# W_down's gradient in parts, the last V turned into other tiles, and the first dO pass inside W_up's gradient

## The chip, the cores and the metric

The kernel runs on one core of a Trainium2 chip. A core has TensorE (PE, matrix products and transposes), VectorE (DVE), ScalarE (ACT), GpSimd (POOL) and SyncE (SP), each with its own instruction queue, and 16 DMA engines that move data between the device's memory and the on-chip memory SBUF. SyncE only issues DMAs; ScalarE and GpSimd issue some too, between their other work. Products land in PSUM, eight banks of which a product of 512 float32 columns fills one. The metric is the device time of one execution in microseconds (us); the median over runs counts.

## The reference

The kernel computes the forward result and eleven gradients of one transformer block (2048 rows of width 512, bfloat16). Cut to what matters:

```
h = layernorm(x) * (1 + ca) + sa             # sa, ca, ga, sb, cb, gb = silu(c) @ w_mod
x = x + ga * A(h)                            # A: 64 segments of 32 rows, 8 memory rows carried on
                                             #    from one segment to the next, 32 heads of 128
h = layernorm(x) * (1 + cb) + sb
x = x + gb * B(h)
B(h) = (sigmoid(h @ w_gate) * (h @ w_up)) @ w_down      # the GLU, inner width 1792
out, vjp = jax.vjp(f, x, mem0, Wq, Wk, Wv, Wo, w_gate, w_up, w_down, c, w_mod)
return out, vjp(grad_out)
```

## The kernel before, in words

The program is one stretch of straight code in stages that follow each other:

- **phase2**: the forward pass over the 64 segments (s = 0 to 63), in order, since each segment's first 8 output rows are the next one's memory. Q, K, V, the turned V, the probabilities and the attention output are stored to DRAM (QST, KST, VT, PS, OT, OSR), for the backward pass. V is turned by a DMA transpose into the one tile `VTr` (L951), except in the last segment, where TensorE turns it in three parts (`turn_v`, L866), VectorE copies the parts to `VTr`, and SP stores it (L990). `RAs` are two pairs of tiles (k and q) that take the projected rows of even and odd segments. At its end, the first rows of the GLU are loaded (`glu_load`).
- **phase3**, first half, the GLU: 16 tiles of 128 rows pass seven stages, s0 to s6, `run_pipeline` with the deepest stage first; so iteration `it` handles stage k of tile it - k, and `after(it)` follows. s0: residual, layernorm, `h2` and `db`. s1: both turned (`hdT`, a DMA transpose from tile 2 on). s2: gate (`sg`) and up (`u`) products, `hh = sg * u`. s3: `du`, `dg`; `hhT` by a DMA transpose. s4: the product with w_down; `duT`, `dgT` by DMA transposes. s5: the gradient of h2, then `da`, `dx1`. s6: sums of gradients, and the turned `da` (`daT`), stored to DAOT. Rows for the weight gradients go to DRAM (HHROWS, DGROWS, DUROWS, DBROWS, H2ROWS). w_down is turned in eight pieces of seven transposes in iteration 2 (`wdT_pieces`).
- W_down's gradient: 14 products `fc` of 128 rows of W_down, each 16 matmuls over the tiles (`wd_chunk`), from `hrs` (columns of HHROWS, three `fc` at a time) and `dbr` (DBROWS). Products 0 to 2 are made in iterations 19 to 21 of the GLU; the rest after it.
- **phase3**, second half: products 3 to 13 of W_down's gradient, then W_gate's and W_up's gradients (32 groups of 16 matmuls). Between them the four weights of the attention are turned, in 32 pieces of 16 transposes (`p4_weights_setup_pieces`, spread by `emit_setup`): a piece is loaded by SP to a staging slot, turned by TensorE into PSUM (`wtp`), and copied by VectorE or ScalarE.
- **phase4**: the backward pass over the segments, from 63 down to 0. Every segment projects dy with WoT (`col_pass`), and turns dO (`dOT`; `dOst` holds its rows). The 8 tail rows of four segments are projected together (`proj_b`, into `RBds`, then turned into `btd`), one group of four ahead; `dO_tails` moves them to rows 96 to 119 of `dOst` by three DMAs on GpSimd's queue.
- **phase5**: the gradients of the attention weights from the stored rows, and the last layernorm backward.

What sets the order. The compiler's planner orders the instructions of each engine and each DMA queue by their place in the program, by its own estimate of when their inputs are there, and it inserts the waits. `self.pin(i0, engines)` fixes the program's order for the instructions recorded since i0 on these engines; `pin_behind` puts them behind an earlier stage. phase2 and the loop of phase4 are fixed on all engines; in the GLU, VectorE is fixed throughout, TensorE and ScalarE up to iteration 2, SP not at all. Tiles are carved out of the same SBUF by pools, stage after stage: a tile of a new stage lies over tiles of earlier ones, and its first write waits until all of these are read for the last time, stores to DRAM included.

Two large tiles, `Wk` and `Wv`, are cut into parts that are used anew after phase2 (`flat`): in `Wk` lie w_gate and w_up, then `dbr` and `hr_0`, then `h2r`; in `Wv` lie w_down and the rings of the GLU's inputs (`ring_a`, `ring_dout`), then the two halves of `ring` with the rows for the weight gradients. WoT, WqT, WkT and WvT, `daq` and `dyT` are allocated from the other end of SBUF.

The loads of the backward loop's first segment, in program order: K and Q rows, the cleared tiles, OT, PS, VT; and then the first dO pass (two halves), `dO_tails`, its turns and the heads' tail columns.

Of the kernel before, what the change touches and what calls it, by code (L numbers as in the profile page):

```python
# [40 lines left out]
class K:  # L41
# [395 lines left out]
    def phase2(self):  # L437
# [15 lines left out]
        with ExitStack() as ctx:  # L453
# [349 lines left out]
            for s in range(NS):  # L803
# [184 lines left out]
                if s == NS - 1:  # L988
                    nc.gpsimd.dma_start(self.w_down, io["B_w_down"].rearrange("(fc p) d -> p fc d", p=128))
                    nc.sync.dma_start(self.VT[s], VTr[:])  # L990
# [86 lines left out]
    def phase3(self):  # L1077
# [9 lines left out]
        with ExitStack() as ctx:  # L1087
# [110 lines left out]
            late = []  # L1198

# [4 lines left out]
            def s2(j, st):  # L1204
                r0, r1 = j * 128, (j + 1) * 128
                hdT = st["hdT"]
                sg = sbp.tile([128, F], BF16, name="sg", bufs=2)
                u = sbp.tile([128, F], BF16, name="u", bufs=1)
# [20 lines left out]
                if j == NT - 1:  # L1229
                    last_hh.append(hh)  # L1230
# [96 lines left out]
            def s6(j, st):  # L1327
# [9 lines left out]
                nc.sync.dma_start(self.DAOT[j * nseg:(j + 1) * nseg].rearrange("s p c t -> p s (c t)"),  # L1337
# [13 lines left out]
            def load_hr(g):  # L1351
                w, n = min(384, F - 384 * g), NT if g else NT - 1
# [3 lines left out]
            last_hh = []  # L1356

            def wd_chunk(fc, ps, ot):
                for j in range(NT):
                    rows = last_hh[0][:, 0:384] if fc < 3 and j == NT - 1 else hrs[fc // 3][:, j, :]  # L1360
                    nc.tensor.matmul(ps[:], lhsT=rows[:, (fc % 3) * 128:(fc % 3) * 128 + 128], rhs=dbr[:, j, :],
                                     start=(j == 0), stop=(j == NT - 1))
# [29 lines left out]
            self.run_pipeline(NT, [first, second, s2, s3, s4, s5, s6], deepest_first=True, after=after)  # L1392
            self.pin(i0, [ET.DVE])
# [9 lines left out]
        with ExitStack() as ctx:  # L1403
# [3 lines left out]
            units = 3 * (FC - 3) + 8 * 2 * NCH * DC  # L1407
            n_setup, done = len(setup_pieces), [0]

            def emit_setup(n):  # L1410
                done[0] += n
                while setup_pieces and (n_setup - len(setup_pieces)) * units < done[0] * n_setup:
                    setup_pieces.pop(0)()
            h2r = self.flat(self.Wk, NT * D, NT * D).rearrange("p (j d) -> p j d", j=NT)
# [23 lines left out]
            for (rows, outw) in ((self.DGROWS, io["out_7"]), (self.DUROWS, io["out_8"])):  # L1438
                for ch in range(NCH):
# [13 lines left out]
                    if outw is io["out_7"] and ch == 0:  # L1453
                        self.get_db(cfg.NS // 4 - 1)
            while setup_pieces:
                setup_pieces.pop(0)()
        self.wvk_ctx.close()

    def p4_weights_setup_begin(self):
# [14 lines left out]
        self.das, self.dbs = {}, {}  # L1474

# [12 lines left out]
    def p4_weights_setup_pieces(self, ctx):  # L1488
# [3 lines left out]
        stg = ctx.enter_context(tc.tile_pool(name="p4stage", bufs=1, reuse_waits="tile"))  # L1492
# [3 lines left out]
        slots = [stg.tile([128, DC * HB * E], BF16, name=f"stage{i}") for i in range(2)]  # L1496
        slots = [t[:, :] for t in slots] + [self.flat(self.Wv, 2 * cfg.NT * 448, DC * HB * E)]
        np_ = [0]

        def slot(pat, **kw):  # L1500
            np_[0] += 1
            return slots[np_[0] % 3].rearrange(pat, **kw)
# [29 lines left out]
        for h0 in range(0, H, HB):  # L1532
            pieces.append(wo_piece(h0))
# [817 lines left out]
```

## Time and profile before

Three runs took 3033.78, 3037.5 and 3036.22 us, a median of 3036.22. The profiled execution took 3034.87 us, of which 3033.1 are the span from the first to the last instruction. Its stages (us from the span's start, borders at TensorE's first instruction of the stage):

| stretch | what | length | TensorE busy | clock |
|---|---|---|---|---|
| 0 to 29.35 | setup | 29.35 | 12.77 | 0.94 |
| 29.35 to 976.16 | phase2, 64 segments | 946.81 | 926.65 | 0.99 |
| 976.16 to 1314.75 | GLU, products 0 to 2 of W_down's gradient | 338.59 | 325.59 | 0.99 |
| 1314.75 to 1361.96 | products 3 to 13 | 47.21 | 43.58 | 0.96 |
| 1361.96 to 1486.41 | W_gate's and W_up's gradients | 124.45 | 124.14 | 1.00 |
| 1486.41 to 2467.73 | phase4, 64 segments | 981.32 | 970.34 | 0.99 |
| 2467.73 to 3033.1 | phase5 | 565.37 | 560.73 | 1.00 |

The clock is the TensorE clock that was granted, as a share of full speed. In the timelines of the prediction, a line has a start, a length, the engine (SPq and ACTq are DMA issues of SP and ScalarE), the source line, the operation, what is written and read, shapes, how many; in brackets the idle time of the engine ahead of it and what ended it. L61 and L63 are the helper that copies out of PSUM. A DMA's length there is its issue, not its transfer.

### The profile page before, as it was taken

Reading aid. Unit: us, or ns where it says so; the run is one execution under the profiler, and the core shown is the slowest. Engines: PE = TensorE matmul, PEld = TensorE weight load, DVE = VectorE, ACT = ScalarE, POOL = GpSimd, SP = SyncE. Lnnn points to the kernel's source line nnn. Section 1 sums busy time; section 2 is a strip of 40 time slices with the busy share of each in tenths; the row PEclk is TensorE's granted clock in tenths of the full one; section 3 lists DMA queues with packets and bytes.
Section 4 is the critical chain, followed back from the end, with each engine's and each line's share of the span. In section 5 each row is a group of like instructions: output and inputs, shape, how many; then the busy total and the mean of one; then the engine's idle time right before and its main releaser. Section 6 shows DMA issues by size and latency. Waiting matters only on the chain.

```text
span 3033.1 us, 106112 instructions
## 1 busy us (share of the span) xinstructions
PE 2963.8 (98%) x44049; PEld 1853.1 (61%) x44049; DVE 1605.2 (53%) x3746; ACT 1288.1 (42%) x3185; POOL 1215.5 (40%) x2643
## 2 busy tenths in 40 slices
PE   6999999999998999999999999999999999999999
PEld 3666666666665544446577777777777754445454
DVE  5566656656655788723355555556555632322230
ACT  2555555555555533312255555555555520101111
POOL 2555555555545222211244444444444422333321
PEclk8999999999999999999999999999999999999999
DMA  9898888898889899988699999999999997766574
GB/s 310 216 222 207 219 214 213 208 213 220 213 210 277 207 229 228 241 243 266 191 243 253 252 248 245 248 243 251 246 248 246 247 279 252 244 203 216 175 242 148
DMA packets 837335, 703.15 MB, mean 232 GB/s; under 512 B 537603, under 2 KB 709811, under 8 KB 835957
## 3 DMA queue, kind: packets, MB, share of 16 engines
q1 hardware_dynamic: 709716, 484.84, 64.1%
q0 software_dynamic: 54544, 148.63, 15.6%
q10 hardware_dynamic: 72592, 62.89, 6.6%
q8 instruction: 346, 5.67, 0.8%
q14 instruction: 137, 1.11, 0.1%
HBM read 295.09 MB, written 276.35 MB: 188 GB/s over the span
## 4 chain that ended last, share of the span: by engine, by line
PE 86%; issue 5%; DMA 4%; DVE 2%; POOL 1%; ACT 1%; SPq 0%; ACTq 0%; POOLq 0%; DVEq 0%
PE pass_ps L255 14%; PE gps L2132 9%; PE dh_ps L215 8%; PE g_ps L1769 6%; PE pass_ps L658 5%; PE gps5o L2147 4%; PE dhq_ps L223 4%; PE at_ps L223 4%; PE gps L1444 3%; PE mm L1286 3%; PE dh_tps L215 3%; PE turn_ps L828 2%; PE dp_ps L1746 2%; PE tps L1677 2%; PE mm L1261 1%
## 5 line engine op out<-in xcount | busy, mean ns | idle before, releaser
L2132 PE MATMUL gps<-rows,hrows 128*128 128x512 bf16 (+2 forms) x2160 | 417.5, 355 | 0.0
L2132 PEld LDWEIGHTS <-hrows 128*128 128x128 bf16 x2160 | 211.3, 98 | 204.5
L61 ACT ACTIVATE ot<-gps 128x512 bf16<-128x512 f32 (+3 forms) x75 | 41.2, 550 | 367.8 <-PE gps L2132 234.2
L1814 POOL COPY dOst<-RAd 96x512 bf16<-96x512 bf16 x128 | 75.4, 613 | 303.2 <-DVE RAd L63 303.2
L658 PE MATMUL pass_ps<-Wv,hT 128*32 128x512 bf16 (+2 forms) x2304 | 188.8, 358 | 0.0
L63 DVE CAST ot<-gps 128x512 bf16<-128x512 f32 (+3 forms) x76 | 48.1, 633 | 261.5 <-PE gps L2132 185.6
L2136 POOL DMA_DIRECT2D out_dram<-ot x108 | 81.3, 753 | 257.3 <-DVE ot L63 142.7
L255 PEld LDWEIGHTS <-hT 128*32 128x32 bf16 x4096 | 125.2, 97 | 94.7 <-DMA Wq<-in_A_Wq_dram 5.0
L1034 POOL TENSOR_TENSOR Pst<-Pst,rden 120x1408 bf16<-120x1408 bf16 x63 | 159.7, 2535 | 51.6 <-issue 29.8
L61 ACT ACTIVATE dVT<-g_ps 128x480 bf16<-128x480 f32 (+1 forms) x192 | 104.7, 545 | 95.3 <-PE g_ps L1769 94.8
L63 DVE CAST Vst<-pass_ps 96x512 bf16<-96x512 f32 x128 | 87.3, 682 | 106.7 <-ACT RBv L61 100.1
L215 PE MATMUL dh_ps<-WvT,dVT 128*32 128x512 bf16 x2048 | 134.3, 382 | 0.2
L255 PE MATMUL pass_ps<-Wq,hT 128*32 128x512 bf16 x2048 | 125.4, 383 | 4.8 <-DMA Wq<-in_A_Wq_dram 4.8
L658 PE MATMUL pass_ps<-Wv,hb 128*32 128x512 bf16 (+2 forms) x636 | 128.7, 353 | 0.0
L255 PE MATMUL pass_ps<-Wk,hT 128*32 128x512 bf16 x2048 | 125.0, 381 | 1.8 <-POOL hT L547 1.1
L223 PE MATMUL at_ps<-Wo,OT 128*32 128x256 bf16 x4096 | 124.4, 274 | 1.9 <-DMA Wo<-in_A_Wo_dram 1.5
L793 POOL DMA_DIRECT2D Vst<-RBv x192 | 99.3, 522 | 60.5 <-ACT ET L840 38.8
L255 PE MATMUL pass_ps<-WoT,dyT 128*32 128x256 bf16 (+1 forms) x3072 | 122.5, 308 | 0.9 <-ACT dyT L1888 0.9
L223 PE MATMUL dhq_ps<-WqT,dQT 128*32 128x256 bf16 x4096 | 122.9, 273 | 0.0
L215 PE MATMUL dh_ps<-WkT,dKT 128*32 128x512 bf16 x2048 | 122.3, 380 | 0.0
L2147 PE MATMUL gps5o<-WoT,rows 128*128 128x512 bf16 x560 | 121.4, 379 | 0.0
L223 PEld LDWEIGHTS <-dQT 128*32 128x32 bf16 x4096 | 109.8, 97 | 15.6
(464 smaller groups left out, 6981.3 us busy)
## 6 DMA issues: line engine op xcount, KB each, us to landing
OSR<-Ost SPq DMA_DIRECT2D x64, 352.0 KB
OT<-OT SPq DMA_DIRECT2D x64, 352.0 KB
VT<-VTr SPq DMA_DIRECT2D x64, 352.0 KB
PS<-Pst SPq DMA_DIRECT2D x64, 352.0 KB
OT_l<-OT SPq DMA_DIRECT2D x64, 352.0 KB
Pst_l<-PS SPq DMA_DIRECT2D x64, 352.0 KB
VT_l<-VT SPq DMA_DIRECT2D x64, 352.0 KB
DVR<-rows_x POOLq DMA_DIRECT2D x64, 352.0 KB, 6.0
```

What stands on the lines that cost most here:

```text
L61: return nc.scalar.activation(out, in_, AF.Copy)
L63: return nc.vector.tensor_copy(out, in_)
L215: self.nc.tensor.matmul(ps[32 * j:32 * j + 32, :], lhsT=lhsT, rhs=w, start=(n < 4), stop=(n >= total - 4), tile_position=(0, 32 * j))
L223: nc.tensor.matmul(ps[32 * j:32 * j + 32, :], lhsT=x[k], rhs=w[k][:, 256 * d:256 * d + 256], start=(n == 0), stop=(n == total - 1), tile_p ...
L255: self.nc.tensor.matmul(ps[32 * j:32 * j + 32, :], lhsT=lhs(c), rhs=rhs, start=(c == 0), stop=(c == DC - 1), tile_position=(0, 32 * j))
L658: nc.tensor.matmul(ps[32 * j:32 * j + 32, o * E:(o + n) * E], lhsT=lhsT, rhs=wc[:, 3 * a + hl:3 * (a + n - 1) + hl + 1:3, :], start=(c == ...
L793: nc.gpsimd.dma_start(Vst[96 + 8 * j:104 + 8 * j, :], rb[32 * j + o:32 * j + o + 8, :])
L1034: nc.gpsimd.tensor_tensor(Pst[0:120, :, :], Pst[0:120, :, :], rden[:, :].unsqueeze(2).to_broadcast([120, G, 128]), op=ALU.mult)
L1286: nc.tensor.matmul(hp[:], lhsT=xT[:, fc, :], rhs=wT[:, fc, :], start=(n == 0), stop=(n == 2 * FC - 1))
L1769: nc.tensor.matmul(ps[:, j, 0:w], lhsT=lh[:, g * GW:(g + 1) * GW], rhs=rh[:, g * GW:g * GW + w], start=True, stop=True)
L2132: nc.tensor.matmul(ps[:, 0:ng * E], lhsT=hrows[:, tp_, c * 128:(c + 1) * 128], rhs=rows[:, tp_, 0:ng * E], start=(tp_ == 0), stop=(tp_ == ...
L2147: nc.tensor.matmul(pss[gg][:], lhsT=rows[:, t, gg * E:(gg + 1) * E], rhs=dyrows[:, t, :], start=(n == 0), stop=(n == NTP - 1))
```

## The change

- phase2, last segment: V's turned parts go to RA0's k and q tiles (free by then) in place of `VTr`, and are stored from there by two DMAs.
- GLU, first iterations: `u` is allocated ahead of `sg`; w_down's pieces use the PSUM buffers of the products for two of four columns, and their copies alternate between ScalarE and VectorE; SP is fixed in the program's order for iterations 0 to 4.
- GLU, last iterations: SP is fixed again from iteration 17 on. `hr_0` and `dbr` are loaded for tiles 0 to 6 (ScalarE's queue, iteration 17) and 7 to 13 (SP, iteration 18), and `dbr` of 14 and 15 in iteration 19. Products 0 to 2 are made in two parts: tiles 0 to 6 and 14 first (two of them in iteration 18, one in 19), then 15 and 7 to 13 (iterations 19, 20, 21); tiles 14 and 15 are taken from SBUF. The results take the `h2` buffers in place of `db`. DAOT of tiles 14 and 15 is stored by GpSimd.
- Attention weights: turned in the order Wq, Wo, Wk, Wv (before: Wo, Wv, Wk, Wq). The staging slots are parts of `Wv` and `Wk` in place of two tiles of their own and one part of `Wv`: for the first four pieces one part of `Wv` and, for the second, a part of `hr_0`; from the fifth on four slots, three of them in `dbr`. SP is fixed in this half too.
- The first dO pass (`first_dO_pass`, `first_dO_turns`) is made inside W_up's gradient, after its first and second groups of columns, with two PSUM banks of its own; its tiles move to the other end of SBUF.
- phase4's start: loads in the order PS, VT, OT (in all segments; VT of segment 63 on ScalarE's queue), then Q; K's tile is cleared and loaded after the first projection, and segment 62's loads are issued there; four clearings move from VectorE to GpSimd or behind.

```diff
+                last_v = [RAs[0]["k"][:, 0:PW], RAs[0]["k"][:, PW:2 * PW], RAs[0]["q"][:, 0:G * GW - 2 * PW]]
...
-                    self.evac("dve", VTr[:, pi * PG:pi * PG + n, :], ps)
+                    self.evac("dve", last_v[pi].rearrange("p (g x) -> p g x", x=GW), ps)
...
-                    nc.sync.dma_start(self.VT[s], VTr[:])
+                    for g0, t, w in ((0, RAs[0]["k"], 8), (8, RAs[0]["q"], G - 8)):
+                        nc.sync.dma_start(self.VT[s, :, g0:g0 + w, :], t[:, 0:w * GW].rearrange("p (g x) -> p g x", x=GW))
...
-                        tp = tp8()
+                        tp = tp8() if c % 4 < 2 else psM.tile([128, 8, 128], BF16, name="tpm", tag="m")
-                        self.evac("dve" if f0 else "act", w_downT[:, c, f0 * 128:(f0 + 7) * 128],
+                        self.evac("dve" if c % 2 else "act", w_downT[:, c, f0 * 128:(f0 + 7) * 128],
...
+                u = sbp.tile([128, F], BF16, name="u", bufs=1)
                 sg = sbp.tile([128, F], BF16, name="sg", bufs=2)
-                u = sbp.tile([128, F], BF16, name="u", bufs=1)
...
-                nc.sync.dma_start(self.DAOT[j * nseg:(j + 1) * nseg].rearrange("s p c t -> p s (c t)"),
+                (nc.sync if j < NT - 2 else nc.gpsimd).dma_start(self.DAOT[j * nseg:(j + 1) * nseg].rearrange("s p c t -> p s (c t)"),
...
+            NA = (NT - 2) // 2
+            def wd_products(fc, ps, js):
+                for j in js:
+                    rows, d = hrs[fc // 3][:, j, :], dbr[:, j, :]
+                    if fc < 3 and j >= NT - 2:
+                        rows, d = last[j][0][:, 0:384], last[j][1][:]
+                    nc.tensor.matmul(ps[:], lhsT=rows[:, (fc % 3) * 128:(fc % 3) * 128 + 128], rhs=d,
+                                     start=(j == 0), stop=(j == NT - 3 if fc < 3 else j == NT - 1))
...
-                if it == NT + 1:
-                    load_hr(0)
-                    nc.scalar.dma_start(dbr, self.DBROWS[:, :].rearrange("(j p) d -> p j d", p=128))
-                elif NT + 3 <= it < NT + 6:
-                    if it == NT + 3:
-                        load_hr(1)
-                    wd_chunk(it - NT - 3, mm(), sbp.tile([128, D], BF16, name="ot2", tag="db", bufs=2))
+                if it == 4:
+                    self.pin(i0, [ET.SP])
+                if it == NT:
+                    parts["i0"] = len(self.traced())
+                elif it == NT + 1 or it == NT + 2:
+                    q, a, b = (nc.scalar, 0, NA) if it == NT + 1 else (nc.sync, NA, NT - 2)
+                    q.dma_start(hr_0[:, a:b, :], self.HHROWS[128 * a:128 * b, 0:384].rearrange("(j p) f -> p j f", p=128))
+                    q.dma_start(dbr[:, a:b, :], self.DBROWS[128 * a:128 * b, :].rearrange("(j p) d -> p j d", p=128))
+                if NT + 2 <= it < NT + 6:
+                    for fc in {2: [0, 1], 3: [2], 4: [], 5: []}[it - NT]:
+                        parts[fc] = mm()
+                        wd_products(fc, parts[fc], [*range(NA), NT - 2])
+                    for fc in {2: [], 3: [0], 4: [1], 5: [2]}[it - NT]:
+                        wd_products(fc, parts[fc], [NT - 1, *range(NA, NT - 2)])
+                        wd_chunk(fc, parts[fc], sbp.tile([128, D], BF16, name="ot2", tag="h2", bufs=2))
+                if it == NT + 3:
+                    nc.sync.dma_start(dbr[:, NT - 2:NT, :], self.DBROWS[128 * (NT - 2):, :].rearrange("(j p) d -> p j d", p=128))
+                    load_hr(1)
...
+                    if outw is io["out_8"] and ch < 2:
+                        self.first_dO_pass(psE, ch)
+                    elif outw is io["out_8"] and ch == 2:
+                        self.first_dO_turns(psE)
...
-        slots = [stg.tile([128, DC * HB * E], BF16, name=f"stage{i}") for i in range(2)]
-        slots = [t[:, :] for t in slots] + [self.flat(self.Wv, 2 * cfg.NT * 448, DC * HB * E)]
+        slots = [self.flat(self.Wv, 2 * NT * 448, n)] + [self.flat(self.Wk, i * n, n) for i in range(3)]
+        first = [slots[0], self.flat(self.Wk, NT * D, n), slots[0], slots[0]]
...
-                    for nm, dram in (("OT", self.OT), ("Pst", self.PS)):
+                    for nm, dram in (("Pst", self.PS), ("VT", self.VT), ("OT", self.OT)):
-                        nc.sync.dma_start(gl3(t), dram[s])
+                        (nc.scalar if s == NS - 1 and nm == "VT" else nc.sync).dma_start(gl3(t), dram[s])
...
+                if s == NS - 1:
+                    nc.gpsimd.memset(Kst_t[:], 0.0)
+                    load_rows(Kst_t, self.KST, s)
+                    for t in (dS, dXTs["dKT"][0], dXTs["dQT"][0]):
+                        nc.gpsimd.memset(gl3(t)[:, :, 120:GW], 0.0)
+                    get_loads(s - 1)
```

The two new functions:

```python
    def first_dO_pass(self, psp, hf):
        t = self.dbs[self.cfg.NS // 4 - 1]
        self.col_pass(psp, self.WoT, hf, lambda c: t[:, c, :, :].rearrange("p s q -> p (s q)"), self.RBd1, ("act", "dve")[hf])

    def first_dO_turns(self, psp):
        self.dO_tails(self.cfg.NS - 1, self.RBd1)
        for hf in range(2):
            self.evac(("act", "dve")[hf], self.btd[:, 4 * hf:4 * hf + 4, :], self.turn_half(psp, self.RBd1, hf)[:])
```

More of the change, by code (lines that the diff above doesn't have):

```diff
@@ L1474, in p4_weights_setup_begin, with dO_tails @@
         self.das, self.dbs = {}, {}
+        firstp = ctx.enter_context(tc.tile_pool(name="p4first", bufs=1, side="right", reuse_waits="tile"))
+        self.RBd1 = firstp.tile([128, 8 * 128], BF16, name="RBd1")
+        self.btd = firstp.tile([128, 8, 128], BF16, name="btd")
+        self.dOst = firstp.tile([128, cfg.G * 128], BF16, name="dOst")
+    def dO_tails(self, s, rows):
+        for j in range(3):
+            o = 32 * j + 8 * (s % 4)
+            self.nc.gpsimd.dma_start(self.dOst[96 + 8 * j:104 + 8 * j, 0:1024], rows[o:o + 8, :])
+    def first_dO_pass(self, psp, hf):
[3 more added lines that the diff above has]
+        self.dO_tails(self.cfg.NS - 1, self.RBd1)
+        for hf in range(2):
+            self.evac(("act", "dve")[hf], self.btd[:, 4 * hf:4 * hf + 4, :], self.turn_half(psp, self.RBd1, hf)[:])
     def get_da(self, t):
```

67 lines of the change are left out of this document (28 added, 39 removed).

## The prediction, made before the changed kernel was run

> **What bounds the kernel now.** I read the page's busy shares first, then the table of stretches around the places that the diff touches, then TensorE's timeline in those places with what it waited for, then the timelines of SyncE, ScalarE and GpSimd there. The page:
>
> ```profile
> PE 2963.8 (98%) x44049; PEld 1853.1 (61%) x44049; DVE 1605.2 (53%) x3746; ACT 1288.1 (42%) x3185; POOL 1215.5 (40%) x2643
> ```
>
> TensorE is the bound: only 69 us of the span are idle, so an edit can win only where TensorE stands still or runs at a lowered clock. The table of stretches (us, then the busy time of each engine, the granted clock, DMA share, GB/s): the end of GLU, the products 3 to 13 of W_down's gradient, the start of GLU, the start of the backward loop, and one ordinary segment of that loop.
>
> ```profile
> 1264.60:1314.75 50.15, 42.57 (x210) 18.42 (x210) 24.59 (x50) 8.73 (x14) 7.41 (x14) 0.97 0.96 253
> 1314.75:1361.96 47.21, 43.58 (x242) 21.37 (x240) 7.76 (x16) 6.46 (x11) 8.38 (x19) 0.96 0.80 252
> 976.16:1026.94 50.78, 45.36 (x348) 26.49 (x349) 32.21 (x51) 30.89 (x46) 14.66 (x28) 1.00 0.87 214
> 1486.41:1512.36 25.95, 18.70 (x321) 12.74 (x324) 12.12 (x28) 8.60 (x21) 11.79 (x26) 0.87 0.61 162
> 1512.36:1527.33 14.97, 14.28 (x298) 10.20 (x301) 8.35 (x21) 8.22 (x21) 6.88 (x17) 1.00 0.96 214
> ```
>
> Four of the five hold idle or slow TensorE; elsewhere (1361.96 to 1486.41, and the loop after 1512.36) it is over 99% busy. The waits, from the timelines (start, length, and in brackets the idle time ahead and its releaser):
>
> ```profile
> 973.90 0.34 SPq L990 DMA_DIRECT2D VT<-VTr  x1
> 980.97 0.54 ACT L1216 ACTIVATE sg<-mm 128x448 bf16<-128x448 f32 x1 [6.78 <-DMA AOA<-at_rb]
> 981.57 0.92 PE L1219 MATMUL mm<-Wk,Wq 128*128 128x448 bf16 x4 [1.46 <-ACT sg L1216]
> 1011.70 0.93 PE L1215 MATMUL mm<-Wk,hdT 128*128 128x448 bf16 x4 [1.60 <-DMA hdT<-h]
> 1257.17 2.81 SPq L1239 DMA_TRANSPOSE hhT<-hh  x1
> 1264.87 2.07 ACTq L1353 DMA_DIRECT2D Wk<-HHROWS  x1
> 1268.41 5.14 SPq L1264 DMA_TRANSPOSE duT<-du  x1
> 1279.44 4.82 SPq L1239 DMA_TRANSPOSE hhT<-hh  x1
> 1280.26 3.19 PE L1286 MATMUL mm<-Wq,duT 128*128 128x512 bf16 x14 [2.81 <-DMA duT<-du]
> 1291.80 4.88 PE L1261 MATMUL mm<-Wv,hhT 128*128 128x512 bf16 x14 [3.48 <-DMA hhT<-hh]
> 1322.67 0.76 DVE L63 COPY WoT<-wtp 128x512 bf16<-128x512 bf16 x2 [3.58 <-DMA out_dram<-ot]
> 1323.15 1.01 PE L1526 MATMUL wtp<-ident,stage 128*128 128x128 bf16 x8 [3.48 <-DVE WoT L63]
> 1486.56 0.34 SPq L1665 DMA_DIRECT2D OT_l<-OT  x1
> 1490.54 1.57 POOL L1695 DMA_DIRECT2D dOst<-RBd  x3 [0.96 <-ACT btd L61]
> 1498.38 0.56 PE L1769 MATMUL g_ps<-Pst_l,dOst 128*128 128x120 bf16 x4 [5.35 <-DMA dOst<-RBd]
> ```
>
> To be seen: the first `sg` of GLU is written 3.9 us after its products could be read; the transposes of tile 14 and 15 take twice as long beside a 3.5 MB load issued at 1264; 14 products after the 3.48 us wait take 4.88 us, where the same take 3.02 elsewhere (granted clock 0.71 in that window); the first weight piece waits for the last stores of GLU; the backward loop waits for the tail rows of dO.
>
> **The change part by part**
>
> *Start of GLU.* Counting tile sizes in program order, `sg` begins 42,400 bytes after Wq's weights and V's turned tile `VTr` ends at 42,624: GLU's first `sg` lies over it and waits for the store issued at 973.90 (landed about 980.9). The change turns the last V into RA0's tiles and puts `u` first; `u` then lies over `VTr` and `ET`, `sg`'s first buffer over the two `Vst`, all read for the last time by 972. `sg` can start at 977, which removes 1.46 + 0.2 us. The store becomes two issues (0.3 us more on SP; only OSR, OT and PS stores queue behind). The eight pieces of w_down's turn get four PSUM buffers and alternate engines, against ScalarE's 3.42 us for four in a row (0.97 us idle); but VectorE, in program order, is held by tile 1's chain until 986.2 (its rows land at 980), so the second VectorE copy ends about 987.5 and of this part I count 1 us. SP in program order up to iteration 4 puts `hdT` of tile 2 ahead of tile 0's `duT` and `dgT` (1.60 us at 1011.70 gone); these two then issue about 8 us later, at 1003, needed at 1018. Late next is VectorE's chain. TensorE idles 5.42 us here; I take 4, ends 1.5 (first wait only) and 5.4.
>
> *End of GLU.* Full-clock work of the stretch: 160 products of 512 columns at 0.216 (28 in 6.04), 16 at 0.189, four sums with turns at 0.55: 39.8. The stretch takes 50.15, so 10.35 can be won. The load is cut: 1.6 MB (7 tiles of HHROWS and DBROWS) on ScalarE's queue at 1264, 1.6 MB on SP behind `hhT` of tile 15, 0.26 MB later; tiles 14 and 15 come from SBUF. Sixteen products move ahead of tile 14's s5, eight more ahead of tile 15's: 5.2 us into the stalls. Walk: s3 of tile 15 ends 1277.3; 16 products to 1280.8; s5 of 14 (its `duT` issued 1268.4, landing by 1277; `dgT` by 1280) to 1287.3; s4 of 15 (`hhT` issued about 1274.5, landing by 1282) to 1290.4; 16 products and sums to 1294.4; s5 of 15 (`duT` issued 1284.3) to 1300.5; 16 products and sums to 1304.5, where product 3 begins, against 1314.75. Its rows load after s4 of 15 (w_down's place), issued 1290.5, 14 us ahead. If the first half lands late, TensorE stands at 1277: 3.5 MB had landed by 1296.5 at the latest, half of it in order by 1280.4, so 3 us at most. SP in program order also puts tile 13's DAOT ahead of `duT` of 15: if the planner places its turn late in s5 of 14 as now (1286.63), `duT` slips about 3 us. DAOT of 14 and 15 (0.37 each on SP) goes to GpSimd (0.54, of 7.4 busy in 50); its readers come in W_gate's gradient. I take 8.5, ends 3 and 10.35.
>
> [...]
>
> *W_down's products 3 to 13.* 11 x 16 x 0.216 + 64 turns x 0.056 = 41.6 of 47.21: 5.6 to win (3.48 wait, the rest clock). Wq's pieces come first; their target lies over Wq's old weights and w_downT, last read by products that end before, so no store is waited for. New: the first piece's slot holds tile 14's and 15's `dout`, free after `ta` of tile 15 (1303.3 in the walk; now 1310.4); 0.5 MB then has 4.7 us until 1308. The fifth to seventh slots lie in `dbr` and open only when product 13 ends, beside a 1.8 MB load: late by up to 3 us. I take 3.5, ends -3 and 5.6.
>
> *Start of the backward loop.* 25.95 against 14.97; 32 products and 8 turns of the first dO pass (2.2 us) move into W_up's gradient with their two copies, two turn copies, three GpSimd issues (1.57, beside a store every 4 us), hidden there. 8.8 can be won. SP's loads still wait for the last product (1486.56); `Pst` first, VT on ScalarE's queue, K and segment 62's loads behind. GpSimd's chain: Qst's clearing 1.27, `dOT` tails 0.76, one issue 0.52, two copies 1.2 = 1490.2 for `dOst`, 1.2 after TensorE could start. Kst's clearing (1.29) and three small ones (0.10 each on VectorE before) come behind; K is needed 7.7 us after. If `Pst` takes 6.58 us like the tail rows did, start is 1493. I take 6.5, ends 4 and 8.
>
> *Edits at nothing.* The loop's load order (OT last, issued at 1512 for use at 1531); GLU's loads no longer run ahead on SP (now those of tiles 2 to 6 by 994), but stay one iteration, 18.8 us, ahead; `dOst`'s clearing (0.65) goes to W_gate's gradient, where VectorE has 39.66 busy of 124; 6.9 KB moved to the right side, so the last stage's second row buffer lies over dQT (free 2471.6, not 2469.1; 1 MB is ahead of it and its product starts 2485).
>
> Sum: 4 + 8.5 + 3.5 + 6.5 = 22.5. The profiled execution took 3034.87 (span 3033.1): 3012.4. It stands 1.35 under the median 3036.22, so 3014. The ends: 5.5 to 29.4, 3031 to 3007.
>
> **The rivals**
>
> *Weight pieces late.* The pieces' slots cost instead of gain: -3 for 3.5, total 16, 3020. For: now a slot is filled 10 us ahead, then it is not. Against: the planner fits turns between products.
>
> *SP's fixed order bites at the end of GLU.* DAOT of 13 holds `duT` and `dgT` of 15: 3 for 8.5, total 17, 3019. For: its turn came at 1286.63.
>
> *Slower: the loop's loads.* In 63 segments OT comes third, with DMA share 0.96 to 1.05. If it lands after VectorE's first product wants it, each segment is longer; from 0.45 us each (28 us) the kernel is slower by over 6, at 0.6 it is 3052. At 0.27 to 0.45 us it is the same. Against: 1.05 MB at 214 GB/s is 5 us, and the loads have 19.
>
> **How the numbers follow.** A measurement tells 0.2%, 6 us. The forecast's own case 0.55 (3007 to 3018), late pieces 0.12, SP's order 0.13: faster 0.80. A loop loss between 0.27 and 0.45 us: same 0.08; above: slower 0.12. The range 3007 to 3031 is the sum of the ends and leaves out the loop's cases.
>
> **What would show it.** Right: `sg` starts within 1 us of its products; product 3 begins 38 to 43 us after s2 of tile 15 ends (now 50.15); no wait over 1.5 us at the first weight piece; `g_ps` 4 to 5 us after the last product of W_up (now 12). Wrong: a segment of the loop longer than 14.97, waits on `wtp` turns, or on `duT` of tile 15.

## The result, and the profile after

The changed kernel takes 3018.78 us (median of 6 runs, 3016.99 to 3021.11) against 3036.35 us before (6 runs, 3030.8 to 3038.52): a ratio of 0.9945 with a 95% interval of 0.9932 to 0.9958, faster by 17.6 us. The forecast of 3014 was 4.8 us too low, and the time lies in its range of 3007 to 3031. The profiled execution took 3019.01 us, with a span of 3017.2 against 3033.1, so 15.9 us are to be found. TensorE is still the bound. The page after:

```profile
PE 2954.9 (98%) x43975; PEld 1851.3 (61%) x44049; DVE 1602.3 (53%) x3743; ACT 1288.9 (43%) x3185; POOL 1215.9 (40%) x2648
```

The table of stretches of the changed kernel (us, then busy time of PE, PEld, DVE, ACT, POOL with counts, granted clock, DMA share, GB/s): GLU's first product to tile 1's s2, the end of GLU, products 3 to 13, W_gate's and W_up's gradients, the start of the backward loop, and one ordinary segment.

```profile
977.00:993.32 16.32, 13.91 (x130) 9.24 (x130) 11.49 (x19) 10.47 (x15) 7.54 (x15) 1.00 0.75 247
1263.75:1306.07 42.32, 40.12 (x205) 18.38 (x209) 24.23 (x50) 8.62 (x14) 7.21 (x13) 1.00 1.01 263
1306.07:1349.95 43.88, 43.29 (x240) 21.22 (x241) 8.65 (x19) 6.46 (x12) 9.48 (x18) 0.96 0.86 277
1349.95:1478.93 128.98, 127.88 (x1000) 76.19 (x1001) 40.59 (x93) 31.00 (x55) 19.54 (x38) 1.00 0.76 244
1478.93:1496.48 17.55, 14.97 (x278) 10.63 (x278) 9.11 (x22) 7.51 (x19) 10.18 (x26) 0.90 0.84 233
1496.48:1511.44 14.96, 14.28 (x296) 10.19 (x293) 8.34 (x21) 8.22 (x21) 6.86 (x17) 1.00 0.95 218
```

The ordinary segment is what it was (14.96, before 14.97). The whole account, with borders at TensorE's first instruction of each stretch:

| stretch | before | after | gain | forecast |
|---|---|---|---|---|
| up to GLU's first product | 976.16 | 977.00 | -0.84 | 0 |
| from there to tile 12's sums | 288.47 | 286.75 | 1.72 | 4 |
| to product 3 of W_down's gradient | 50.12 | 42.32 | 7.80 | 8.5 |
| products 3 to 13 | 47.21 | 43.88 | 3.33 | 3.5 |
| W_gate's first product to the second segment's dO pass | 150.33 | 146.53 | 3.80 | 6.5 |
| the rest | 1520.81 | 1520.72 | 0.09 | 0 |

The first line can't be told from scatter: GLU's first product stood anywhere from 975.6 to 980.1 in the runs below, with the same code ahead of it. So kernels are compared by stretches here; a single time of theirs (3016.7 to 3028.3 us) holds that 4.5 us too.

The timeline of the changed kernel where TensorE still waits, with the DMA issues and copies behind it (start, length, engine, line, what, idle ahead and its releaser):

```profile
977.96 0.54 ACT L1220 ACTIVATE sg<-mm 128x448 bf16<-128x448 f32 x1 [2.92 <-PE mm L1219]
987.52 0.55 PE L1128 MATMUL tp<-ident,Wv 128*128 128x128 bf16 x7 [2.31 <-DVE w_downT L63]
1267.53 5.61 SPq L1268 DMA_TRANSPOSE duT<-du  x1
1275.06 3.30 SPq L1243 DMA_TRANSPOSE hhT<-hh  x1
1280.52 3.19 PE L1290 MATMUL mm<-Wq,duT 128*128 128x512 bf16 x14
1281.34 0.36 SPq L1341 DMA_DIRECT2D DAOT<-daT  x1
1283.73 6.05 SPq L1268 DMA_TRANSPOSE duT<-du  x1
1286.56 3.18 PE L1265 MATMUL mm<-Wv,hhT 128*128 128x512 bf16 x14
1305.14 0.40 PE L1337 MATMUL tp<-ident,da 128*128 128x128 bf16 x4 [1.78 <-DVE da L1322]
1306.07 3.46 PE L1368 MATMUL gps<-Wk,Wv 128*128 128x512 bf16 x9
1366.20 0.62 DVE L63 CAST ot<-gps 128x448 bf16<-128x448 f32 x1 [2.99 <-DMA out_dram<-ot]
1367.20 0.38 PE L1563 MATMUL wtp<-ident,Wv 128*128 128x128 bf16 x4 [0.80 <-DVE WqT L63]
1483.36 0.37 PE L1801 MATMUL g_ps<-Pst_l,dOst 128*128 128x120 bf16 x4 [1.52 <-DMA Pst_l<-PS]
```

To be seen: `sg` no longer holds TensorE (it is written as soon as its products are there, at 977.96), but w_down's turn now waits 2.31 us for VectorE, where it waited 0.97 us for ScalarE. The transposes of tiles 14 and 15 are still issued slowly (5.61 and 6.05 us), but the products that need them start without a wait; what is late at the end of GLU is `da` of tile 15. The weight pieces of W_q come without a wait on their loads, but one copy stands behind a store on VectorE. At the loop's start `Pst` is late, by 1.52 us instead of 5.35 us for the tail rows.

### The profile page after: what moved, and what is told of

It is laid out like the page before. It is cut to its first block, busy times and chain, and to the rows that moved or that the text cites. A ratio compares the mean times of both kernels' runs of the same rounds, so it can differ in the third digit from the quotient of the medians.

```text
span 3017.2 us, 106054 instructions
## 1 busy us (share of the span) xinstructions
PE 2954.9 (98%) x43975; PEld 1851.3 (61%) x44049; DVE 1602.3 (53%) x3743; ACT 1288.9 (43%) x3185; POOL 1215.9 (40%) x2648
## 4 chain that ended last, share of the span: by engine, by line
PE 90%; issue 4%; DMA 2%; DVE 2%; POOL 1%; ACT 1%; SPq 0%; DVEq 0%; POOLq 0%; ACTq 0%
PE pass_ps L255 14%; PE gps L2170 11%; PE dh_ps L215 8%; PE g_ps L1801 6%; PE pass_ps L658 5%; PE gps5o L2185 4%; PE dhq_ps L223 4%; PE at_ps L223 4%; PE mm L1290 3%; PE gps L1469 3%; PE dh_tps L215 3%; PE turn_ps L828 2%; PE dp_ps L1778 2%; PE tps L1721 2%; PE mm L1250 2%
```

## The experiments

Each kernel is the changed one with one edit, if nothing else is said. (Where an edit adds or takes lines, the line numbers behind it shift by a few.) The table has the stretches of one profiled execution of each, in us:

- A: GLU's first product to tile 1's s2
- B: tile 12's sums to product 3
- C: products 3 to 13
- D: W_gate's first product to the first segment's pass over dyT
- E: from that pass to the first `g_ps`
- F: from that pass to the second segment's

| kernel | A | B | C | D | E | F |
|---|---|---|---|---|---|---|
| before | 17.15 | 50.12 | 47.21 | 128.37 | 8.05 | 22.83 |
| after | 16.32 | 42.32 | 43.88 | 128.98 | 4.43 | 18.42 |
| whole products | 17.95 | 43.46 | 42.36 | 128.81 | 4.33 | 17.32 |
| whole load | 17.90 | 47.72 | 42.07 | 129.26 | 4.61 | 18.49 |
| late parts | 16.67 | 41.63 | 42.16 | 129.07 | 4.40 | 17.64 |
| second half behind | 15.96 | 40.63 | 43.33 | 129.13 | 4.44 | 17.38 |
| w_down's turn as before | 15.03 | 42.32 | 42.32 | 129.83 | 4.41 | 17.50 |
| no order on SP | 19.27 | 42.33 | 42.22 | 129.12 | 4.52 | 17.49 |
| W_o first | 16.16 | 42.33 | 48.64 | 129.29 | 4.42 | 17.72 |
| three store buffers | 18.07 | 42.33 | 42.16 | 128.28 | 4.67 | 20.91 |
| dO pass at the loop | 16.38 | 42.32 | 42.12 | 129.14 | 5.12 | 18.99 |
| dO pass and loads | 16.58 | 42.33 | 42.27 | 129.11 | 7.30 | 21.55 |
| OT first | 16.59 | 42.32 | 42.33 | 128.93 | 5.66 | 19.30 |
| three together | 15.79 | 41.61 | 42.17 | 128.60 | 4.70 | 20.67 |

B repeats within 0.02 us where its code is the same. A, C and F do not; the last section shows the granted clock at these places. D and E together lie between 133.14 and 134.24 in the seven kernels with the same code there, so a difference below 1 us in them shows nothing.

### The end of GLU: the cut of the load, or the products moved ahead?

**Whole products.** The load stays cut, products 0 to 2 are made whole, as before:

```diff
-                    for fc in {2: [0, 1], 3: [2], 4: [], 5: []}[it - NT]:
-                        parts[fc] = mm()
-                        wd_products(fc, parts[fc], [*range(NA), NT - 2])
                     for fc in {2: [], 3: [0], 4: [1], 5: [2]}[it - NT]:
-                        wd_products(fc, parts[fc], [NT - 1, *range(NA, NT - 2)])
+                        parts[fc] = mm()
+                        wd_products(fc, parts[fc], [*range(NA), NT - 2, NT - 1, *range(NA, NT - 2)])
```

> Stretch from tile 12's sums to product 3 of W_down's gradient (50.1 us before, 42.3 after). Theory: the cut load alone lets the transposes of tiles 14 and 15 land in time; the 24 products that were moved ahead fill nothing, and only rob the end of cover. Then with the three sums whole and in the drain, no wait on duT, dgT or hhT over 0.5 us appears, the 1.78 us wait for da of tile 15 goes, and the stretch is 40 to 41.2 us. Rival (the prediction's walk): the moved products fill stalls of 5.2 us; without them waits on duT, dgT and hhT come back and the stretch is 44 to 47 us.

B was 43.46: between the two. The timeline of this kernel, in the form of the one above:

```profile
1276.63 1.67 PE L1290 MATMUL mm<-Wq,duT 128*128 128x512 bf16 x7
1280.81 8.88 SPq L1268 DMA_TRANSPOSE duT<-du  x1
1289.11 1.67 PE L1368 MATMUL mm<-Wk 128*128 128x512 bf16 x7 [0.62 <-DMA Wk<-DBROWS]
1292.92 3.19 PE L1290 MATMUL mm<-Wq,duT 128*128 128x512 bf16 x14 [1.48 <-DMA duT<-du]
1304.80 0.39 PE L1337 MATMUL tp<-ident,da 128*128 128x128 bf16 x4
1307.43 3.61 PE L1368 MATMUL gps<-Wk,Wv 128*128 128x512 bf16 x16 [0.73 <-ACT ot L61]
```

Tile 14's s5 starts right behind s3 of tile 15, with no wait: the 16 products that the change puts there fill nothing. But tile 15's `duT` is issued 2.9 us earlier (1280.81 against 1283.73), right behind the second half of the load; its issue is 8.88 us long (6.05 in after), and TensorE waits 1.48 us for it. The 1.78 us for `da` is gone. So the theory held for tile 14 and the rival, in small, for tile 15. The earlier issue is not the whole reason: it ends at 1289.69, against 1289.78 in after. What differs is TensorE, which in after comes to these products only at 1293.69, because the parts of products 0 to 2 lie ahead of them. There the moved parts do cover a wait. Two small waits lengthen B as well: 0.62 us for rows of `dbr`, and 0.73 us for a copy at product 3.

**Whole load.** The opposite half: the parts stay, the load is one piece again.

```diff
-                elif it == NT + 1 or it == NT + 2:
-                    q, a, b = (nc.scalar, 0, NA) if it == NT + 1 else (nc.sync, NA, NT - 2)
+                elif it == NT + 1:
+                    q, a, b = nc.scalar, 0, NT - 2
```

> The first 14 tiles' rows of HHROWS and DBROWS in one pair of loads on ScalarE's queue, as long before as the first half now; the products stay in parts. Theory: the bytes that lie beside the transposes decide when they land; duT or dgT of tile 14 or hhT of tile 15 are late again, the products moved ahead cover 3.5 us of it, and the stretch is 44 to 46.5 us (42.3 after). Rival: the moved products and SyncE's fixed order carry the gain, wherever the load stands: 42 to 43 us.

B was 47.72, worse than either expected, and 5.4 us more than after. But what waited was not a transpose; it was the moved products, for their own rows, and their clock was lowered behind the wait (7 products in 3.17 us, where they take 1.67). Waits are about 3.5 of the 5.4 us (2.90 here, 0.58 at product 3), the rest is nearly all clock. The load in one piece without the moved products was not tried, so how the 7.8 us divide between the two edits is known only with the other one in place: 5.4 for the cut, 1.1 for the moved products.

```profile
1283.49 3.17 PE L1368 MATMUL mm<-Wk 128*128 128x512 bf16 x7 [2.90 <-DMA Wk<-HHROWS]
```

**Late parts.** The first halves behind tile 15's s4, all second halves behind its s5:

```diff
-                    for fc in {2: [0, 1], 3: [2], 4: [], 5: []}[it - NT]:
+                    for fc in {2: [], 3: [0, 1, 2], 4: [], 5: []}[it - NT]:
...
-                    for fc in {2: [], 3: [0], 4: [1], 5: [2]}[it - NT]:
+                    for fc in {2: [], 3: [], 4: [], 5: [0, 1, 2]}[it - NT]:
```

> The first halves of products 0 to 2 of W_down's gradient behind tile 15's s4, all second halves behind tile 15's s5. From tile 12's sums to product 3: 42.32 us after, 43.46 with the products whole. Theory: the first halves were never needed as cover ahead of tile 14's s5, since its transposes have landed; behind s4 they cover the transposes of tile 15, and 24 products (5.2 us) behind s5 cover the 5.4 us that da of tile 15 takes, so the wait of 1.78 us falls to 0.5 or less: 40.2 to 41.2 us, and no lowered clock behind it. Rival: tile 15's duT is issued while the second half of the load is under way, as with whole products, and lands late: a wait of 1 to 2 us there, 41.5 to 43 us in all.

B was 41.63, 0.4 over the theory's range. Both mechanisms are there: 24 products now cover `da`'s chain (no wait for it), and tile 15's `duT` is issued behind the second half again (8.93 us) and waited for, 0.83 us:

```profile
1293.38 3.19 PE L1290 MATMUL mm<-Wq,duT 128*128 128x512 bf16 x14 [0.83 <-DMA duT<-du]
```

B and C together take 83.79 against 86.20 after, of which some 1.6 are the lowered clock that after had in C.

**Second half behind.** The late parts, and the second half of the load in iteration 19, behind tile 15's `duT` and `dgT`:

```diff
-                elif it == NT + 1 or it == NT + 2:
+                elif it == NT + 1 or it == NT + 3:
```

> As the run with the late parts, and the second half of the load behind tile 15's duT and dgT on SyncE. From tile 12's sums to product 3: 41.63 us with the late parts. Theory: duT of tile 15 took 8.93 us to issue because that half lay beside it; behind it the issue takes 2.4 to 4 us, the wait of 0.83 us is gone and the stretch is 40.4 to 41.0 us. Rival: the rows of the second half, or those of product 3 that are loaded behind them, are now late: a new wait of 1 us or more and 41.6 us or more up to product 3, or up to W_gate's first product more than the 83.8 us of the run with the late parts.

Tile 15's `duT` on SP's queue in this kernel:

```profile
1281.76 2.39 SPq L1268 DMA_TRANSPOSE duT<-du  x1
```

`duT` takes 2.39 us to issue where it took 8.93, the wait is gone and B is 40.63, as the theory had it. The rival was right on what follows: the rows that are loaded behind that half are now late (in C, waits of 0.46 us for a group of HHROWS and of 0.64 us for DGROWS), B and C together are 83.96, and nothing is won over the late parts. In this pair of runs load and transpose stand on one queue. In before they stood on two, and the issue was long there as well: SP's `duT` of tile 14 took 5.14 us from 1268.41, behind a load that ScalarE had issued from 1264.19 to 1266.94 (2.81 for `hhT` at 1257.17, ahead of that load).

### The start of GLU

**w_down's turn as before**: two PSUM buffers, four copies on ScalarE, then four on VectorE.

```diff
-                        tp = tp8() if c % 4 < 2 else psM.tile([128, 8, 128], BF16, name="tpm", tag="m")
+                        tp = tp8()
-                        self.evac("dve" if c % 2 else "act", w_downT[:, c, f0 * 128:(f0 + 7) * 128],
+                        self.evac("dve" if f0 else "act", w_downT[:, c, f0 * 128:(f0 + 7) * 128],
```

> w_down's turn with two PSUM buffers, four copies on ScalarE and then four on VectorE, as before; all else as after. From GLU's first product to the first product of tile 1's s2: 17.15 us before, 16.32 after. Theory: the alternating copies stand behind tile 1's chain in VectorE's program order and cost the new 2.31 us wait; without them that wait goes, the old 0.97 us wait on ScalarE comes back, and the stretch is 15.2 to 15.8 us. Rival: the turn's copies are bound by the two engines however they are dealt out: 16.2 us or more.

A was 15.03, under the theory's range and the shortest of all. Its timeline:

```profile
987.77 0.55 PE L1128 MATMUL tp<-ident,Wv 128*128 128x128 bf16 x7 [0.66 <-ACT w_downT L61]
988.15 0.54 PE L1250 MATMUL mm<-w_downT,Wq 128*128 128x448 bf16 x2
990.21 2.64 DVE L63 COPY w_downT<-tp 128x896 bf16<-128x896 bf16 x4
```

The four copies of the first half are done on ScalarE, one behind the other, before VectorE is free of tile 1's chain, and tile 0's products with w_down (L1250) begin between the later turns. With the alternating copies half of that first half waits for VectorE. So this part of the change cost 1.3 us of what the rest had won here, by this pair of executions. A scatters: at full clock it was 15.96 to 16.67 in four kernels with the alternating copies (the wait was 1.96 to 2.67 us), and 15.03 and 15.79 in the two with the old ones, so the cost is about 0.9 us on average.

**No order on SP** for iterations 0 to 4:

```diff
-                if it == 4:
-                    self.pin(i0, [ET.SP])
```

> SyncE's program order up to iteration 4 left out; all else as after. From the first product of tile 1's s2 to the steady GLU (the product at 1235.8 in after): 243.34 us before, 242.45 after and in three other runs with that order. Theory: the order is what puts hdT of tile 2 ahead of duT and dgT of tile 0; without it the 1.60 us wait at tile 2's s2 comes back and the stretch is 243.2 to 243.5 us. Rival: the planner orders them well now that sg starts earlier: 242.4 to 242.6 us.

Both missed. The wait at tile 2's s2 did not come back; another, larger one came, and GLU up to tile 12's sums took 296.61 us against 286.75:

```profile
998.97 3.92 SPq L1243 DMA_TRANSPOSE hhT<-hh  x1
1010.36 0.61 PE L1265 MATMUL mm<-Wv,hhT 128*128 128x512 bf16 x1 [5.80 <-DMA hhT<-hh]
```

Without the order the planner puts five tiles' reads of AOA, with their other inputs, ahead of tile 0's `hhT` on SP's queue, where after has three; `hhT` goes out at 998.97 instead of 990.74, and its product stands until 1010.36. The five reads alone are not the reason: before has five there as well, and its `hhT`, issued at 994.78, was waited for only until 1000.71. Why this `hhT` took 11.4 us from its issue to its product, against 5.9 there, is not shown. From tile 1's s2 on GLU is 6.9 us longer than in after (277.34 against 270.43, which repeats within 0.1 us); the other 2.95 us lie in A, in a longer wait at w_down's turn (3.90 us against 2.31) and a lowered clock, and A scatters. Before had no such order either and took 271.32 us there, so against before the order is worth 0.89 us.

### The weight pieces

**W_o first**, as before, in the new slots:

```diff
-        for (src_ap, dst) in ((io["A_Wq"], self.WqT), (None, None), (io["A_Wk"], self.WkT), (io["A_Wv"], self.WvT)):
+        for (src_ap, dst) in ((None, None), (io["A_Wq"], self.WqT), (io["A_Wk"], self.WkT), (io["A_Wv"], self.WvT)):
```

> W_o's two pieces ahead of W_q's, as before, in the new slots. Products 3 to 13 of W_down's gradient: 47.21 us before, 43.88 after. Theory: WoT lies over tiles of GLU whose last stores are still under way, so the first copy waits for them, TensorE for it, 2.5 to 3.5 us, and some at a lowered clock behind it: 46.2 to 48 us. Rival: what helped is the slots filled earlier or the shorter drain, not the order: 43.5 to 44.5 us.

C was 48.64, and the wait is the one of before (3.48 there), on the copy into WoT:

```profile
1317.76 0.71 PE L1576 MATMUL wtp<-ident,Wv 128*128 128x128 bf16 x8 [3.11 <-DVE WoT L63]
```

The theory holds; C went over its range by lowered clocks on both sides of the wait (0.57 in the first 4 us of C, 0.64 and 0.50 in the 4 us behind the wait). The order of the pieces carries this part's gain.

**Three store buffers** for the gradients:

```diff
-            op_ = ctx.enter_context(tc.tile_pool(name="p3g_o", bufs=2, reuse_waits="tile"))
+            op_ = ctx.enter_context(tc.tile_pool(name="p3g_o", bufs=3, reuse_waits="tile"))
```

> Three store buffers in place of two for the gradients of W_down, W_gate and W_up; all else as after. From W_gate's first product to the first segment's pass over dyT: 128.98 us after, 128.81 to 129.83 in the other runs with the new weight pieces, of which 0.6 to 1.3 us are one wait for a copy into WqT. Theory: VectorE waits there for a store to free its buffer while the pieces' loads crowd the DMA engines, and the copies of W_q's turn stand behind it; with a third buffer that wait is under 0.2 us and the stretch 127.9 to 128.5 us. Rival: the copy is late for its own piece's sake: 128.8 us or more.

No wait on a copy into WqT is left, and D is 128.28, where the kernels with two buffers took 128.81 to 129.83: the theory. In after VectorE stood idle for 2.99 us until a store had freed its buffer (1366.20 above), and the weight copies behind it.

### The start of the backward loop

**dO pass at the loop**, as before; the new order of loads and clearings stays:

```diff
-                    if outw is io["out_8"] and ch < 2:
-                        self.first_dO_pass(psE, ch)
-                    elif outw is io["out_8"] and ch == 2:
-                        self.first_dO_turns(psE)
...
+            for hf in range(2):
+                proj_b(NS // 4 - 1, hf)()()
+            self.dO_tails(NS - 1, self.RBd1)
+            turn_b(NS // 4 - 1)()
             to_heads("pool", btd[:], 0, 8, 32, 8, 24)
```

> The first dO pass, its turns and the tail rows at the start of the backward loop, as before; all else as after. From W_gate's first product to the second segment's pass over dyT: 151.20 us before, 147.40 after (146.1 to 147.8 in the runs so far). Theory: what was won is the tail rows' trip through GpSimd's queue and DMA that TensorE waited for; with the pass back at the loop's start that wait is there again (3 to 5.4 us) and the stretch is 150 to 151.5 us. Rival: the gain comes from the new order of loads and clearings at the loop's start, and the pass costs the same wherever it stands: 147 to 148.5 us.

D and F together are 148.13, the rival's: putting the pass back costs little. F holds a lowered clock in some runs, so D and E are the cleaner sum: 134.26, against 133.41 after (133.14 to 134.24 with the same code) and 136.42 before. The tail rows are waited for, but for 2.43 us:

```profile
1483.67 0.55 PE L1801 MATMUL g_ps<-Pst_l,dOst 128*128 128x120 bf16 x4 [2.43 <-DMA dOst<-RBd]
```

**dO pass and loads**: the same, and the second segment's three loads ahead of it as well (`get_loads(NS - 2)` in front of the two passes).

> The dO pass at the start of the loop as before, and the second segment's three loads ahead of it too, as before; all else as after. From W_gate's first product to the second segment's pass over dyT: 151.20 us before, 147.40 after, 148.13 with the dO pass alone back at the loop. Theory: bulk loads that were issued ahead of the tail rows made their trip long (4.7 us behind the last issue before, 2.7 to 3.4 with those loads behind); with both back the wait at the first g_ps is 4.5 to 5.5 us again and the stretch is 150 to 151.5 us. Rival: the loads don't touch it; what had made the trip long was GpSimd's queue with K's clearing in it, which stays behind here: 147.8 to 148.6 us.

D and F together are 150.66, in the theory's range. D and E together are 136.41, the value of before, and most of the wait is back:

```profile
1486.23 0.56 PE L1802 MATMUL g_ps<-Pst_l,dOst 128*128 128x120 bf16 x4 [4.60 <-DMA dOst<-RBd]
```

GpSimd issues the three tail DMAs at the same place in both (from 1478.76 and 1479.14, right behind the turn's copies), with K's clearing behind them in both. So it is the 1 MB of loads for the next segment in front of them that makes the trip long: 2.15 of the 3.0 us that D and E won come from issuing these loads later. The other 0.85 would be the place of the pass, but that is no more than the scatter of D and E, so a gain from it is not shown. The pass moved with the loads left ahead was not tried.

**OT first** in the loop's loads, all segments:

```diff
-                    for nm, dram in (("Pst", self.PS), ("VT", self.VT), ("OT", self.OT)):
+                    for nm, dram in (("OT", self.OT), ("Pst", self.PS), ("VT", self.VT)):
```

> Loads of the backward loop in the order OT, Pst, VT, as before; all else as after. Theory: the order is worth nothing in an ordinary segment (14.96 to 14.98 us, as before and after) because each load has more than 10 us of slack; at the loop's start Pst lands one 352 KB transfer later, and the stretch from the first to the second segment's pass over dyT is 18.8 to 20.5 us (17.3 to 18.5 in the runs with Pst first). Rival (the slower case of the prediction): OT third is late; then OT first makes a segment shorter than with OT third by 0.05 us or more, and the loop of 62 segments by over 3 us.

E is 5.66 against 4.43, by a wait of 2.75 us for `Pst`; an ordinary segment is 14.97 (1496.86 to 1511.83), as with OT third. The order matters at the start and nowhere else.

### The three edits that won, together

Late parts, w_down's turn as before, three store buffers.

> The late parts, w_down's turn copied as before and the third store buffer together, on top of after. Theory: the three lie in different stretches and add up: to tile 1's s2 15.0 to 15.8 us (16.32 after), from tile 12's sums to W_gate's first product 83.5 to 84.3 us (86.20 after), from there to the first segment's pass 128.0 to 128.6 us (128.98 after); together 3.5 to 5 us off after's 3018.8, so 3013.5 to 3015.5 us and a ratio to before of 0.992 to 0.994. Rival: what is won at the start is taken back by the wait for the next tile's rows, and what is won at the end by lowered clocks behind waits that are left; then 3017.5 us or more.

Each stretch came out as the theory had it (A 15.79, B and C 83.78, D 128.60), but the time did not: 3017.28 us (5 runs, 3016.65 to 3019.12), a ratio to before of 0.9953 (0.9939 to 0.9966). That can't be told from the 0.9945 of the changed kernel. It lies above the theory's 3013.5 to 3015.5 and just short of the rival's 3017.5. In its profiled execution F took 20.67, with the clock at 0.50 from about 1482.2 to 1488.9: 2.25 us more than after's 18.42, two thirds of the 3.3 us won elsewhere. That is the rival's mechanism, lowered clocks behind a wait that is left, at another place than it named. The kernel before, measured beside this one, had a median of 3032.27 (9 runs), 4.1 us below the one measured beside after, so the two times can't be set against each other directly. Why the rest of the gain is missing was not settled.

## Why the prediction was right, and where it was wrong

**The sum.** Forecast 22.5, found 16.65 in the four stretches and 0.75 lost outside them. Two terms carry the miss: the start of GLU (2.3 too much) and the start of the loop (2.7). All four signs named for right came: `sg` right behind its products, product 3 after 42.32 us, no wait at the first weight piece, `g_ps` after 4.43 us. One sign named for wrong came too, in small: a wait of 0.80 us on a weight piece's turn.

**Start of GLU: 4 forecast, 1.7 found.** The first `sg` followed its products at once, as said, and the 1.60 us wait at tile 2 is gone. Two terms are mis-sized. The larger one is w_down's turn: the prediction saw VectorE held until 986.2 and its second copy ending at 987.5, and still counted 1 us of gain. TensorE resumed at 987.52, behind just that copy: a loss, 1.3 us in the run with the old copies and 0.9 on average. The other is the SP order, counted with 1.6 us: from tile 1's s2 to tile 12's sums 0.89 us was won (271.32 to 270.43), since waits of 0.81 and 1.15 us for ScalarE's copies, at 1001.88 and 1018.79, now stand where 0.41 and 0.20 stood. No run undoes V's new tiles or `u`'s place alone, so the first wait's gain rests on the trace.

**End of GLU: 8.5 forecast, 7.8 found.** The cut of the load did what was said. The walk itself comes to 10.25, of which the prediction took 8.5 without a term for what would be lost, so that 8.5 lies near 7.8 is partly luck. The walk failed in its last step, "16 products and sums to 1304.5": 16 products are 3.5 us, and `da` of tile 15 takes 5.4 us from the end of s5 (1299.74) to the turn (1305.14), a chain on VectorE that the walk has no term for. The step that put 5.2 us of products "into the stalls" was mostly idle: with the load cut there are no stalls at tile 14, and at tile 15 the parts cover 1.48 us for `duT` and 0.62 us for rows. The rival of SP's order didn't bite: DAOT of tile 13 was issued at 1281.34, and `duT` of tile 15 behind it, at 1283.73, came when its buffer was free (tile 14's products with it ended then). The transposes did not stay at their landings of before: `hhT` of tile 15 was used without a wait at 1286.56, where TensorE had waited 3.48 us for it, until 1291.80.

**Products 3 to 13: 3.5 forecast, 3.3 found.** This execution ran the first nine products at a lowered clock. The ten other kernels with the same order of pieces, and with product 3's rows loaded as in after, took 42.1 to 42.4, a gain of 4.8 to 5.1, near the upper end of 5.6. The rival of late pieces fell: no wait on a piece's load.

**Start of the loop: 6.5 forecast, 3.8 found.** `g_ps` came 4.43 us behind W_up's last product, inside the 4 to 5 that were given. The step that failed is "2.2 us move into W_up's gradient ..., hidden there": that stretch grew by 4.53 us (124.45 to 128.98). The loop's start itself became 8.3 us shorter (25.88 to 17.55), near the 8.8 that could be won, so the 2.2 that should have been 4.53 is nearly the whole miss. The pass and its turns took 3.3 there (1.9, 0.98 and 0.45, the first half in three bits between weight turns), and 1.1 are waits for copies, most of them behind the store. With the pass back at the loop's start the stretch is 125.22, and the pass takes 3.92 there: TensorE pays for it nearly the same in both places. The reason was wrong in part too: the tail rows were late because of the loads ahead of them, and the same gain, but for 0.85 us that lies within the scatter, was to be had without moving the pass.

**The slower case** fell: OT third in 63 segments costs nothing, 14.96 against 14.97.

**Not undone alone**: DAOT's stores on GpSimd, the clearings that moved, VT's load on ScalarE's queue and the new slots of the weight pieces. What each is worth stays open.

## What to carry to other kernels

When a stall is covered in two ways at once, undo each alone: here the cut of the load made most of the products moved into the stall useless there, and they were missing at the end, under a chain on VectorE. Before a copy is given to an engine that is fixed in program order, look when that engine is free; an idle share says nothing of it. A small transfer that is waited for should be issued ahead of the large ones that are not: at the loop's start here that was worth 2.15 us (D and E together 134.26 against 136.41).

## What the runs showed of the hardware

A wait's price was not its length alone here. The same 1.78 us wait for `da` (with 0.20 more behind two short groups) stands in the kernels with B of 42.32 and 42.33 alike; in the four microseconds behind it the granted clock differs. The table of stretches, after and w_down's turn as before:

```profile
1306.07:1310.07 4.00, 3.78 (x14) 1.51 (x12) 0.81 (x2) 0.60 (x2) 3.31 (x6) 0.58 0.93 306
```

```profile
1307.94:1311.94 4.00, 4.00 (x29) 2.11 (x26) 1.15 (x3) 0.60 (x2) 3.31 (x6) 1.00 0.93 287
```

The granted clock, third from the end, is 0.58 and 1.00; in W_o first it was 0.57. It fell behind this wait in two of the eight kernels with B of 42.32 or 42.33. In after, in stretches of 1 us, it was 0.84, then 0.50 three times, then 0.95: half speed for 3.4 us, from about 1306.7 to 1310.1. That cost 1.6 us (C 43.88 against 42.2), nearly as much as the wait. The other places go the same way: behind the wait in w_down's turn the clock fell at 2.56 and 2.68 us (A 17.95 and 18.07) and stayed at 2.16, 2.31 and 2.67 (in four more kernels it was low from A's start on, behind three waits of about 0.5 us each within 2.6 us; A 16.4 to 17.9); at the loop's start it fell in four of ten kernels behind a wait of 1.5 to 1.7 us (F 18.4 to 20.9) and not in the others, behind 1.4 to 1.6 us (17.3 to 17.7). There the slow stretch lasted 3.4 us in after (granted clock 0.50 from 1484.2 to 1487.6), and about 7 us in before (0.50 from 1496.9 to 1503.7), in three store buffers and in the three together (24 products of `dh_ps` in 2.75 us in both, where late parts took 1.48).

Waits of 1.52 us (for `Pst`) and 1.78 us (for `da`) were followed by a clock of 0.50 in after, and waits of 1.60 us (for `Pst`, no order on SP), 1.79 us (for `da`, w_down's turn as before) and 2.67 us (w_down's turn, late parts) were not. What decides between them is not shown. So two kernels whose work differs by 2 or 3 us at such places can't be ranked by one execution. A wait of 1.5 to 2 us cost between its own length and, by the largest F (20.9 against 17.4, behind 1.70 us), an estimated 5 us.
